# The rows of a main job are turned and split earlier, and the table of flexible jobs is built one job later

## The chip, the cores and the metric

One core of one Trainium2 chip. The metric is the device time of one execution in microseconds (us); lower is better.

## The reference

`x` is 8 x 1856 x 256. First comes a spectral layer: `X = rfft(x, axis=1)`, a complex product with `w_r + i w_i` plus biases, a soft threshold of 0.01 on the real and imaginary part, and `irfft` back to 14,848 rows of 256. Then a mixture of experts: every row picks a group of 4 and an expert in it (argmax of two small products, 16 experts in all), and its output is

```
h = np.maximum(xg[mask_e] @ w1[g, e], 0.0)      # 256 -> 1024
ye = h @ w2[g, e]                               # 1024 -> 256
out[tok_idx] = combined[:, None] * ye           # product of two softmax weights
```

## The kernel before

The spectral layer runs over four pairs of batches on TensorE, with transposes on VectorE (DVE). Each finished row is routed and scattered by GpSimd (POOL) into a list per expert in device memory, `xs_d`. Part of the experts' work (the early jobs, 256 rows each) is interleaved with the end of the spectral layer. The order of TensorE, ScalarE (ACT) and DVE there is written by hand: a string `ORDER` whose letters are steps. `D` is a second product of an early job, `E` and `J` are its output steps on ACT and DVE (lines 873 and 878), `K` the store.

After that string come 39 main jobs (`JOBS`, line 20) in one Python loop (line 1143). Three engines run in exactly the order in which the program emits their instructions; the order of the sync engine (SP), which issues the loads, is set by a scheduler. A job is one expert's rows: "l" has 384 rows, "e" 512 rows, "f" (flexible) 128 rows of an expert chosen at run time, "h" (half) two times 64 rows of two experts. Jobs 0 to 4 are l, l, l, e, l. Jobs 5, 8, 14, 23, 26, 32 and 36 are flexible; 11, 17, 29 and 35 are half jobs.

Every fp32 operand is a sum of two fp32r parts (high, low). A job goes through these steps:

- Its rows `xg` are loaded by SP (line 452). DVE turns them in 32 x 32 blocks into `x32` (line 455; the rows of the trace call this tile `x`), one buffer. `prep` then makes the high part `xth` on ACT (line 474) and the low part `xtl` on DVE (line 475). For a half job `x32` is used as it is. All this is emitted at the end of the job before (line 1191), after that job's `drain(rest)`.
- First product: `up_g` (line 480) for e and l jobs, eight slices `f` of six matmuls each (line 487). After each slice ACT makes `hh` (line 491) and DVE `hl` (line 493). Flexible jobs use `flex_mm` (line 500), with ACT's `ht`, and `flex_tr` (line 513), which turns `ht` on TensorE in two halves; ACT and DVE take `hh` and `hl` (lines 520 and 521) from it. Half jobs use `half_mm` and `half_tr` in the same way, with a plain copy on DVE (line 1099).
- Second product: `down_g` (line 545), 16 matmuls per 128 rows (lines 556 and 557), then ACT (563), DVE (564) and a store by POOL (543). It is emitted during the next job: the first two blocks of 128 rows before the next job's first product, a third or fourth one (`rest`) after it or, in flexible and half jobs, in halves between the turns.
- Meanwhile the weights of a coming job are split into high and low, eight pieces, one after each slice `f` (`todo`, lines 431 on ACT and 432 on DVE). The raw weights are loaded into two tiles `xt` (line 419); a load waits until the pieces of the tile before are done.

Which expert a flexible or half job has is written in `tab`, with the rows left in `left_of`, by `flex_table` (line 923): some 60 small DVE operations, six transposes on TensorE (line 1017), copies (1018), three small products (1029). It is a generator; four of its steps are drawn after each slice `f` of an l or e job, from job 0 on. SP reads `tab` with register loads before it can load a flexible job's weights (line 1048).

Of the kernel before, what the change touches and what calls it, by code (L numbers as in the profile page):

```python
# [10 lines left out]
F32 = mybir.dt.float32  # L11
# [18 lines left out]
NB, S, D = 8, 1856, 256  # L30
# [19 lines left out]
NF = 4  # L50
# [3 lines left out]
JOBS = _jobs()  # L54
# [103 lines left out]
def spectral_moe(ctx: ExitStack, tc: tile.TileContext, x, wri, bri, wgate, w1, w2, cst, out):  # L158
# [135 lines left out]
    def ids_of(pool, xi, w, bufs):  # L294
        both = pool.tile([128, 8], F32, name="si", bufs=bufs)
        si, gate = both[:, 4:4 + w].bitcast(I32), both[:, 0:w]
        nc.vector.tensor_scalar_add(out=si, in0=xi[:, 0:w, 0], scalar1=OFF)
        nc.vector.tensor_copy(out=gate, in_=xi[:, 0:w, 1])
        return Ids(gate, si)
# [21 lines left out]
    def bank():  # L321
        return pa.tile([128, 512], F32, name="bank")
# [32 lines left out]
    def drain(gen):  # L355
        for _ in gen:
            pass
# [103 lines left out]
    def turned(xg, n):  # L461
        xt = xq.tile([128, 2, 512], F32, name="x32", bufs=1)
        for c in range(0, n, 256):
            m = min(256, n - c)
            turn_rows(xt[:, :, c:c + m], xg, c // 32, (c + m) // 32)
        return xt

    def prep(xg, n):
        xt = turned(xg, n)
        xth = xq.tile([128, 2, 512], F32R, name="xth")  # L470
        xtl = xq.tile([128, 2, 512], F32R, name="xtl")
        for c in range(0, n, 256):
            ts = slice(c, min(n, c + 256))
            nc.scalar.copy(out=xth[:, :, ts], in_=xt[:, :, ts])  # L474
            nc.vector.tensor_tensor(out=xtl[:, :, ts], in0=xt[:, :, ts], in1=xth[:, :, ts].bitcast(F32), op=ALU.subtract)  # L475
        return xth, xtl
# [339 lines left out]

    @steps_of(range(len(jobs)))
    def e_ids(n):
        ids[n] = ids_of(early["mp"], xgs[n][1], 2, 2 * NF)

    @steps_of(range(len(jobs)))
    def e_turn(n):
# [35 lines left out]
    @steps_of(range(len(jobs)), range(2), range(2))  # L858
    def down_mm(n, t, half):
        if half == 0:  # L860
            psum["d", n, t] = early["py"].tile([128, 512], F32, name="py") if n < 2 else bank()
        o, ts = psum["d", n, t], slice(t * 128, (t + 1) * 128)
        w2b, w2h = views(wts[jobs[n][1]])[2:]
        for f in range(half * 4, half * 4 + 4):
            hh, hl = hid[n, f // 2 * 2]
            nc.tensor.matmul(o, lhsT=hh[:, f % 2, ts], rhs=w2b[:, :, f, :], start=f == 0, stop=f == 7, skip_group_check=True)
            nc.tensor.matmul(o[:, 0:D], lhsT=hl[:, f % 2, ts], rhs=w2h[:, f, :], start=False, stop=f == 7,
                             skip_group_check=True)
# [13 lines left out]
    def down_out(n, t):  # L882
# [6 lines left out]
        G=g_mm, H=g_turn, R=route_steps(), S=scatter_steps(), W=w_high, V=w_low, I=e_ids, F=e_fetch, T=e_turn, X=e_high,  # L889
        Y=e_low, U=up_mm, A=up_high, B=up_low, D=down_mm, E=down_act, J=down_add, K=down_out)  # L890

    ms = ExitStack()
    with ExitStack() as ph:
        done = 0
        ms.enter_context(tc.manual_schedule(engines=engines))
        for c in ORDER.replace("\n", ""):
            next(steps[c])
            done += c == "o"
            if c == "o" and done == NP * K1:
                fwd.close()  # L900
                early["mp"] = ph.enter_context(tc.tile_pool(name="mp", bufs=1))
                yp.append(ph.enter_context(tc.tile_pool(name="yp", bufs=3)))
                early["hp"] = ph.enter_context(tc.tile_pool(name="hp", bufs=6))
                early["pp"] = ph.enter_context(tc.tile_pool(name="pp", bufs=2, space=PSUM))
                early["py"] = ph.enter_context(tc.tile_pool(name="py", bufs=1, space=PSUM))
        assert not pend and all(next(g, None) is None for c, g in steps.items() if c not in "yzS")
        held = {e: views(wts[e]) for e in HELD}
    inv.close()

# [9 lines left out]
    nflex = ft.tile([1, 1], I32, name="nflex")  # L919
    tab = ft.tile([1, 6, 128], I32, name="tab")  # L920
    left_of = ft.tile([128, 3, 128], F32, name="left_of")

    def flex_table():
        ones_f = ft.tile([128, 128], F32, name="ones_f")
# [86 lines left out]
        yield  # L1011
        nc.vector.tensor_copy(out=nflex, in_=kk[0:1, 0:1])
        yield from (None,) * 9
        for i in range(0, 6, 2):
            o = pg.tile([128, 512], F32, name="pg")
            for c in range(2):
                nc.tensor.transpose(o[0:1, c * 128:c * 128 + 128], tb[:, i + c:i + c + 1], ident)
            nc.vector.tensor_copy(out=tab[:, i:i + 2, :], in_=o[0:1, 0:256].rearrange("p (c k) -> p c k", c=2))
            yield
        o = pg.tile([128, 512], F32, name="pg")  # L1020
        dgs = []
        for c in range(3):
# [22 lines left out]
        return xg, xi, left_k  # L1045

    def flex_entry(i, k):
        return (nc.values_load(tab[:, 2 * i, k], engines=sp, min_val=0, max_val=NE - 1),
                nc.values_load(tab[:, 2 * i + 1, k], engines=sp, min_val=0, max_val=NE * CAP))

# [14 lines left out]
    def flex_ids(rows):  # L1065
# [10 lines left out]
            tb = t.bitcast(I32)  # L1076
            nc.vector.tensor_tensor(out=tb, in0=tb, in1=k, op=ALU.bitwise_and)
        return xg, ids_of(xq, xi, 1, 4)

    def half_prep(xg):  # L1080
        return turned(xg, 128)

    def half_mm(xt, wt, hts):
        for q in range(2):
# [46 lines left out]
        s0, n = (0, EARLY) if kind == "e" else (EARLY, STAT - EARLY)  # L1131
        return (*fetch(xq, q, s0, n, 2, 4), n)

    def prep_job(j, xg, n):
        return half_prep(xg) if JOBS[j][0] == "h" else prep(xg, n)

    dma_next()
    table = flex_table()
    with ms:
        prev = None  # L1140
        xg, jids[0], n = rows_of(0)
        x2 = prep_job(0, xg, n)
        for i, (kind, q) in enumerate(JOBS):
            ids, n = jids[i], jids[i].n * 128
            if kind in "el" and i not in jw:
                jw[i] = jw[i - 1] if JOBS[i - 1] == ("e", q) else held[q]
            wt = jw[i]
            if i + 2 < len(JOBS) and JOBS[i + 2][0] == "h":
                k = JOBS[i + 2][1] + KF - KH
                jw[i + 2], rows[i + 2] = half_load(slice(k, k + 1))  # L1150
            nxt = rows_of(i + 1) if i + 1 < len(JOBS) else None
            if nxt:
                jids[i + 1] = nxt[1]
            rest = iter(())
            if prev is not None:
                if prev[3] == "h":
                    half_down(prev[0], prev[1], prev[2], "out")
                else:
                    down(psy, "py", prev[0][0], prev[1][0], prev[2], "out")
                    if len(prev[1]) > 1:  # L1160
                        rest = down_g(psy, "py", prev[0][1], prev[1][1], prev[2], "out")
            todo = []
            if i in split_at:
                jw[split_at[i]], todo = split_w(raws.pop(split_at[i]))
            hts = []
            if kind == "h":
                hs = hq.tile([128, 8 * 256 + 64], F32, name="hh")[:, 0:8 * 256].rearrange("p (f t) -> p f t", f=8)
                drain(half_mm(x2, wt, hts))
                next(rest, None)
                half_tr(hts[0], 0, hs)  # L1170
                next(rest, None)
                half_tr(hts[1], 1, hs)
            elif kind == "f":
                hs = h_tiles(n)
                for _ in flex_mm(x2, wt, hts):
                    emit(todo, 2)
                flex_tr(hts[0], 0, hs[0])
                next(rest, None)
                flex_tr(hts[1], 1, hs[0])
            else:  # L1180
                hs = h_tiles(n)
                for _ in up_g(psh, x2, n, wt, hs):
                    emit(todo, 1)
                    drain(islice(table, 4))
            emit(todo, len(todo))
            if i in split_at:
                dma_next()
            drain(rest)
            prev = (hs, ids if kind == "h" else [ids.cut(c, min(c + 2, ids.n)) for c in range(0, ids.n, 2)], wt, kind)
            if nxt is not None:  # L1190
                x2 = prep_job(i + 1, nxt[0], nxt[2])
        for h2, ids in zip(prev[0], prev[1]):
            down(psy, "py", h2, ids, prev[2], "out")

    nfx = nc.values_load(nflex[:, 0:1], min_val=0, max_val=128)  # L1195
    with tc.For_i(KF, nfx, 1) as iv:
        rw, rw_rows = flex_load(bass.ds(iv, 1))
        wt, todo = split_w(rw)
        emit(todo, len(todo))
        hts, hs = [], h_tiles(128)  # L1200
        xg, ids = flex_ids(rw_rows)
        drain(flex_mm(prep(xg, 128), wt, hts))
        for q in range(2):
            flex_tr(hts[q], q, hs[0])
        down(psy, "py", hs[0], ids, wt, None)
        wt, rw_rows = half_load(bass.ds(iv, 1))
        hts, h = [], hq.tile([128, 8 * 256 + 64], F32, name="hh")[:, 0:8 * 256].rearrange("p (f t) -> p f t", f=8)
        xg, ids = flex_ids(rw_rows)
        drain(half_mm(half_prep(xg), wt, hts))
        for q in range(2):  # L1210
            half_tr(hts[q], q, h)
        half_down(h, ids, wt, None)
# [37 lines left out]
```

## Time and profile before

| | us |
|---|---|
| median of 3 runs (1189.3 to 1198.6) | 1190.08 |
| the profiled execution | 1195.48 |
| its span in the trace | 1193.6 |
| TensorE busy in the span | 1149.6 (96%) |
| DVE busy | 791.7 (66%) |
| ACT busy | 672.9 (56%) |

The profiled execution is 1.9 us longer than its span, and 0.45% above the median. The main jobs take the time from 551 us to the end. Matmuls overlap, and their ends are modelled, so a step between two starts says more than one duration. [...]

### The profile page before, as it was taken

The page shows a single profiled execution, that of the slowest core. Times are in us where ns is not written, and L with a number is a line of the kernel's source. Part 1 is how long each engine was busy: PE and PEld are TensorE (multiplying, and loading weights), DVE is VectorE, ACT ScalarE, POOL GpSimd, SP SyncE. Part 2 cuts the span into 40 slices and gives each one's busy share as a digit, 9 for nine tenths or more (in the row PEclk, how much of TensorE's full clock was granted, in tenths as well). Part 3 has the DMA queues.
Part 4 walks back from the last instruction along what each step waited for, and adds up shares of the span by engine and source line. Part 5 has one row for each costly group of instructions (what it writes and reads, how often), then busy time and mean ns, then how long its engine had stood idle before and what let it go on. Part 6 is the DMA issues. An engine that isn't in the chain of part 4 may idle for free. (4 is left out here: it accounts for less than half of the span.)

```text
span 1193.6 us, 20882 instructions
## 1 busy us (share of the span) xinstructions
PE 1149.6 (96%) x7428; PEld 990.6 (83%) x7428; DVE 791.7 (66%) x1806; ACT 672.9 (56%) x1506; POOL 261.9 (22%) x257
## 2 busy tenths in 40 slices
PE   8999999999999889998899999999999999999997
PEld 5988889897889569887889888888898898798776
DVE  4449676978787778845785845846767566475542
ACT  2777867685778565534364734634546455454432
POOL 1000013503533532561112111111111111111101
PEclk9999999999999999999999999999999999999989
DMA  9872114103311255443353554454434356455200
GB/s 387 327 279 85 37 34 139 66 1 118 118 38 38 66 135 136 142 145 95 96 177 120 150 202 133 120 230 130 121 113 135 110 174 195 118 177 195 102 10 28
DMA packets 114602, 155.82 MB, mean 131 GB/s; under 512 B 89274, under 2 KB 90045, under 8 KB 104000
## 3 DMA queue, kind: packets, MB, share of 16 engines
q1 hardware_dynamic: 95616, 104.33, 28.7%
q0 software_dynamic: 12048, 30.67, 6.9%
q10 hardware_dynamic: 6832, 19.47, 4.2%
q8 instruction: 59, 0.97, 0.3%
q14 instruction: 47, 0.39, 0.1%
HBM read 104.47 MB, written 52.46 MB: 131 GB/s over the span
## 5 line engine op out<-in xcount | busy, mean ns | idle before, releaser
L556 PE MATMUL py<-big,hh 128*128 128x512 f32 x824 | 289.6, 394 | 0.0
L487 PE MATMUL ph<-xth,big 128*128 128x384 f32 (+1 forms) x896 | 255.5, 361 | 4.0 <-ACT xth L474 3.4
L543 POOL DMA_INDIRECT out_dram<-yo,si x123 | 119.8, 974 | 568.7 <-DVE yo L564 497.2
L557 PE MATMUL py<-big,hl 128*128 128x256 f32 x824 | 230.4, 280 | 2.5 <-DVE hl L493 2.3
L277 POOL DMA_INDIRECT xs_d<-v,sloti x128 | 138.7, 1084 | 338.9 <-ACT xh L649 154.6
L493 DVE SCALAR_TENSOR_TENSOR hl<-ph,hh 128x256 fp32r<-128x256 f32 x448 | 151.7, 380 | 62.0 <-ACT hh L491 59.7
L487 PEld LDWEIGHTS ph<-xth,big 128*128 128x128 f32 x896 | 165.7, 189 | 22.5 <-ACT xth L474 6.2
L556 PEld LDWEIGHTS py<-big,hh 128*128 128x128 f32 x824 | 154.5, 187 | 35.8 <-issue 3.2
L491 ACT ACTIVATE hh<-ph 128x256 fp32r<-128x256 f32 x448 | 133.9, 352 | 78.3 <-PE ph L487 74.7
L487 PE MATMUL ph<-xtl,big 128*128 128x384 f32 (+1 forms) x448 | 162.2, 362 | 2.6 <-DVE xtl L475 2.6
L557 PEld LDWEIGHTS py<-big,hl 128*128 128x128 f32 x824 | 155.5, 189 | 4.0 <-DVE hl L493 2.9
L563 ACT ACTIVATE yo<-py,si 128x256 f32<-128x256 f32 x103 | 48.8, 473 | 151.5 <-PE py L557 146.8
L564 DVE SCALAR_TENSOR_TENSOR yo<-py,si,yo 128x256 f32<-128x256 f32 x103 | 49.5, 482 | 109.5 <-ACT yo L563 108.2
L679 PE MATMUL pw<-wh,xh 128*128 128x256 f32 x480 | 120.2, 292 | 0.0
L432 DVE TENSOR_TENSOR big<-xt,big 128x512 fp32r<-128x512 f32 x168 | 114.1, 682 | 0.0
L679 PE MATMUL pw<-wl,xh 128*128 128x256 f32 x480 | 113.5, 278 | 0.0
L431 ACT CAST big<-xt 128x512 fp32r<-128x512 f32 x168 | 103.7, 621 | 0.0
L487 PEld LDWEIGHTS ph<-xtl,big 128*128 128x128 f32 x448 | 84.6, 189 | 12.8 <-DVE xtl L475 5.3
L679 PEld LDWEIGHTS pw<-wh,xh 128*128 128x128 f32 x480 | 90.8, 189 | 2.8 <-issue 2.4
L679 PEld LDWEIGHTS pw<-wl,xh 128*128 128x128 f32 x480 | 90.7, 189 | 2.6 <-issue 2.4
L692 DVE TENSOR_TENSOR big<-rp,rn 128x512 f32<-128x512 f32 x60 | 42.0, 705 | 45.1 <-ACT rp L686 34.2
L636 PEld LDWEIGHTS pg<-CF,big 128*128 128x128 f32 x480 | 63.8, 198 | 8.5 <-issue 2.7
(200 smaller groups left out, 2034.5 us busy)
## 6 DMA issues: line engine op xcount, KB each, us to landing
xt<-in_w_dram SPq DMA_DIRECT2D x50, 1024.0 KB
xs_d<-zero ACTq DMA_DIRECT2D x16, 1170.0 KB
big<-in_w_dram SPq DMA_DIRECT2D x16, 1024.0 KB
xt<-in_x_dram SPq DMA_DIRECT2D x8, 1024.0 KB
xg<-xs_d SPq DMA_DIRECT2D x64, 96.0 KB
xg<-xs_d SPq DMA_DIRECT2D x48, 128.0 KB
big<-in_x_dram SPq DMA_DIRECT2D x4, 1024.0 KB
v<-in_x_dram SPq DMA_DIRECT2D x4, 1024.0 KB
```

The source lines that it names most:

```text
L277: ins = nc.gpsimd.indirect_dma_start(out=xs_d, out_offset=bass.IndirectOffsetOnAxis(ap=sl_, axis=0), in_=row, in_offset=None, bounds_check ...
L431: nc.scalar.copy(out=wt[:, 2 * i, cs], in_=raws[i][:, cs])
L432: nc.vector.tensor_tensor(out=wt[:, 2 * i + 1, cs], in0=raws[i][:, cs], in1=wt[:, 2 * i, cs].bitcast(F32), op=ALU.subtract)
L487: nc.tensor.matmul(o[:, :n], lhsT=a_[:, ch, fs], rhs=b_[:, ch, 0:n], start=k == 0, stop=k == 5)
L491: nc.scalar.activation(out=hh[:, f, :m], in_=ov, func=AF.Relu)
L493: nc.vector.scalar_tensor_tensor(out=hl[:, f, :m], in0=ov, scalar=0.0, in1=hh[:, f, :m].bitcast(F32), op0=ALU.max, op1=ALU.subtract)
L543: ins = nc.gpsimd.indirect_dma_start(out=out, out_offset=bass.IndirectOffsetOnAxis(ap=ids.si[:, t:t + 1], axis=0), in_=ysb, in_offset=None ...
L556: nc.tensor.matmul(o, lhsT=hh[:, f, ts], rhs=w2b[:, :, f, :], start=f == 0, stop=f == 7, skip_group_check=True)
L557: nc.tensor.matmul(o[:, 0:D], lhsT=hl[:, f, ts], rhs=w2h[:, f, :], start=False, stop=f == 7, skip_group_check=True)
L564: nc.vector.scalar_tensor_tensor(out=ysb, in0=o[:, 0:D], scalar=gate_w, in1=ysb, op0=ALU.mult, op1=ALU.add)
L636: nc.tensor.matmul(o[:, m * 128:(m + 1) * 128], lhsT=zys[pr][:, k, ch * 128:(ch + 1) * 128, bt], rhs=T_v[:, k, :], start=True, stop=True)
L679: nc.tensor.matmul(y[:, bt * D:(bt + 1) * D], lhsT=a_[:, bt * 2 + ch, cs], rhs=w_[:, ri, ch, :], start=False, stop=fin, skip_group_check=True)
```

## The change

1. `prep` is taken apart into `turned` (DVE's turn) and `parts` (`xth`, `xtl`).
2. The last two output steps of the early jobs (`EJKEJK`) are cut off from the string and emitted after job 0's turn and split. The products that they read lie in `pg` banks now.
3. In a flexible job the next job's turn is emitted after `flex_mm`, and its split between the two `flex_tr`. In a half job both are emitted after `half_mm`.
4. `flex_table` is drawn from job 1 on instead of job 0; two copies of `tab` instead of three.

```diff
-    def prep(xg, n):
-        xt = turned(xg, n)
+    def parts(xt, n):
         xth = xq.tile([128, 2, 512], F32R, name="xth")
...
-            psum["d", n, t] = early["py"].tile([128, 512], F32, name="py") if n < 2 else bank()
+            psum["d", n, t] = (early["py"].tile([128, 512], F32, name="py") if n < 2 else
+                               pg.tile([128, 512], F32, name="pg") if n == len(jobs) - 1 else bank())
...
+    order = ORDER.replace("\n", "")
+    tail = order.rindex("D") + 2
+    assert order[tail - 1:] == "KEJKEJK"
...
-        for c in ORDER.replace("\n", ""):
+        for c in order[:tail]:
...
-        for i in range(0, 6, 2):
+        for i, n in ((0, 4), (4, 2)):
             o = pg.tile([128, 512], F32, name="pg")
-            for c in range(2):
+            for c in range(n):
...
-    def prep_job(j, xg, n):
-        return half_prep(xg) if JOBS[j][0] == "h" else prep(xg, n)
+    def prep_job(j, xt, n):
+        return xt if JOBS[j][0] == "h" else parts(xt, n)
...
-        x2 = prep_job(0, xg, n)
+        x2 = prep_job(0, turned(xg, n), n)
+        for c in order[tail:]:
+            next(steps[c])
...
-            hts = []
+            hts, x2n = [], None
             if kind == "h":
...
                 drain(half_mm(x2, wt, hts))
+                x2n = prep_job(i + 1, turned(nxt[0], nxt[2]), nxt[2])
                 next(rest, None)
...
                 for _ in flex_mm(x2, wt, hts):
                     emit(todo, 2)
+                xt = turned(nxt[0], nxt[2])
                 flex_tr(hts[0], 0, hs[0])
+                x2n = prep_job(i + 1, xt, nxt[2])
                 next(rest, None)
...
                     emit(todo, 1)
-                    drain(islice(table, 4))
+                    drain(islice(table, 4 if i else 0))
...
             if nxt is not None:
-                x2 = prep_job(i + 1, nxt[0], nxt[2])
+                x2 = prep_job(i + 1, turned(nxt[0], nxt[2]), nxt[2]) if x2n is None else x2n
```

What this moves at three places. First DVE at the end of the early jobs, before:

```order
L855 SCALAR_TENSOR_TENSOR hl<-ph,hh 128x512 x4
L878 SCALAR_TENSOR_TENSOR yo<-bank,si,yo 128x256 x4
L297 TENSOR_SCALAR si<-xi 128x3
L298 COPY si<-xi 128x3
L455 STREAM_TRANSPOSE x_6837<-xg 128x8x2x32
L455 STREAM_TRANSPOSE x_6837<-xg 128x4x2x32
L475 TENSOR_TENSOR xtl<-x_6837,xth 128x2x256
L475 TENSOR_TENSOR xtl<-x_6837,xth 128x2x128
L297 TENSOR_SCALAR si<-xi 128x3
```

and the same place now (`x_6837` and `x_6825` are job 0's `x32`; lines are those of the changed file, one or a few off):

```order
L854 SCALAR_TENSOR_TENSOR hl<-ph,hh 128x512 x4
L878 SCALAR_TENSOR_TENSOR yo<-bank,si,yo 128x256 x2
L297 TENSOR_SCALAR si<-xi 128x3
L298 COPY si<-xi 128x3
L455 STREAM_TRANSPOSE x_6825<-xg 128x8x2x32
L455 STREAM_TRANSPOSE x_6825<-xg 128x4x2x32
L474 TENSOR_TENSOR xtl<-x_6825,xth 128x2x256
L474 TENSOR_TENSOR xtl<-x_6825,xth 128x2x128
L878 SCALAR_TENSOR_TENSOR yo<-pg,si,yo 128x256 x2
L297 TENSOR_SCALAR si<-xi 128x3
```

Job 0's turn and low part have moved ahead of the last two outputs.

Second, DVE in the first flexible job (job 5), whose successor is job 6; before:

```order
L564 SCALAR_TENSOR_TENSOR yo<-py,si,yo 128x256 x2
L521 TENSOR_TENSOR hl<-ph,hh 128x4x128 x2
L564 SCALAR_TENSOR_TENSOR yo<-py,si,yo 128x256
L455 STREAM_TRANSPOSE x_8034<-xg 128x8x2x32 x2
L475 TENSOR_TENSOR xtl<-x_8034,xth 128x2x256 x2
```

and now:

```order
L563 SCALAR_TENSOR_TENSOR yo<-py,si,yo 128x256 x2
L455 STREAM_TRANSPOSE x_7995<-xg 128x8x2x32 x2
L520 TENSOR_TENSOR hl<-ph,hh 128x4x128
L474 TENSOR_TENSOR xtl<-x_7995,xth 128x2x256 x2
L520 TENSOR_TENSOR hl<-ph,hh 128x4x128
L563 SCALAR_TENSOR_TENSOR yo<-py,si,yo 128x256
```

The turn stands ahead of the first `hl`, the low part between the two. ACT's two `xth` moved in the same way between its two `hh`.

Third, ACT from the last half job (35) over flexible job 36 to job 37; before:

```order
L1091 ACTIVATE ht<-ph 128x512 x2
L563 ACTIVATE yo<-py,si 128x256
L431 CAST big<-xt 128x512 x8
L474 CAST xth<-x_13378 128x2x128
L1108 ACTIVATE yo<-py,si 128x256
L509 ACTIVATE ht<-ph 128x512 x2
L520 CAST hh<-ph 128x4x128 x2
L474 CAST xth<-x_13450 128x2x256 x2
```

and now (`x_13325` is job 36's, `x_13434` job 37's):

```order
L1095 ACTIVATE ht<-ph 128x512 x2
L473 CAST xth<-x_13325 128x2x128
L562 ACTIVATE yo<-py,si 128x256
L431 CAST big<-xt 128x512 x8
L1112 ACTIVATE yo<-py,si 128x256
L508 ACTIVATE ht<-ph 128x512 x2
L519 CAST hh<-ph 128x4x128
L473 CAST xth<-x_13434 128x2x256 x2
L519 CAST hh<-ph 128x4x128
```

Job 36's high part went ahead of the eight pieces of job 37's weights.

## Rows read from the trace of the kernel before

**Rows 1.** The page: busy time by engine, and granted clock in 40 slices.

```profile
PE 1149.6 (96%) x7428; PEld 990.6 (83%) x7428; DVE 791.7 (66%) x1806; ACT 672.9 (56%) x1506; POOL 261.9 (22%) x257
...
PEclk9999999999999999999999999999999999999989
```

**Rows 2.** Timeline, start of job 0: start us, us, engine, line, tiles [idle before, releaser].

```profile
551.46 0.48 DVE L878 SCALAR_TENSOR_TENSOR yo<-bank,si,yo 128x256 f32<-128x256 f32 x1 [2.32 <-ACT yo L873]
...
552.00 1.03 DVE L455 STREAM_TRANSPOSE x<-xg 128x512 f32<-128x512 f32 x2
...
553.39 1.03 DVE L475 TENSOR_TENSOR xtl<-x,xth 128x512 fp32r<-128x512 f32 x2 [0.36 <-ACT xth L474]
...
553.71 0.44 PE L487 MATMUL ph<-xth,big 128*128 128x384 f32 x1 [2.80 <-ACT xth L474]
```

**Rows 3.** Windows: stretch, us, busy PE PEld DVE ACT POOL, PEclk, DMA share, GB/s.

```profile
538.00:545.00 7.00, 5.77 (x39) 5.28 (x40) 2.54 (x4) 2.16 (x4) 0.53 (x1) 1.00 0.65 126
553.70:557.60 3.90, 3.57 (x11) 3.32 (x12) 1.40 (x7) 1.06 (x3) 0.00 (x0) 0.56 0.71 136
557.60:564.10 6.50, 6.50 (x39) 6.50 (x38) 6.29 (x29) 6.00 (x18) 0.00 (x0) 1.00 0.00 0
599.70:604.00 4.30, 4.30 (x26) 3.92 (x25) 3.66 (x10) 2.56 (x8) 0.00 (x0) 1.00 0.69 244
...
1134.40:1141.30 6.90, 5.96 (x16) 4.67 (x16) 1.02 (x5) 1.75 (x4) 0.97 (x1) 0.51 0.01 3
```

**Rows 4.** Timeline, DVE and TensorE, job 0's first product and the second after it.

```profile
557.06 0.62 DVE L493 SCALAR_TENSOR_TENSOR hl<-ph,hh 128x256 fp32r<-128x256 f32 x2 [2.50 <-ACT hh L491]
...
569.06 0.67 DVE L493 SCALAR_TENSOR_TENSOR hl<-ph,hh 128x256 fp32r<-128x256 f32 x2
...
564.14 0.39 PE L556 MATMUL py<-big,hh 128*128 128x512 f32 x1
...
567.76 0.39 PE L557 MATMUL py<-big,hl 128*128 128x256 f32 x1 [1.12 <-DVE hl L493]
...
569.53 0.39 PE L557 MATMUL py<-big,hl 128*128 128x256 f32 x1 [1.15 <-DVE hl L493]
```

**Rows 5.** Timeline, DVE in job 2, slices that split weights without table steps.

```profile
597.62 0.61 DVE L493 SCALAR_TENSOR_TENSOR hl<-ph,hh 128x256 fp32r<-128x256 f32 x2
...
602.14 0.62 DVE L493 SCALAR_TENSOR_TENSOR hl<-ph,hh 128x256 fp32r<-128x256 f32 x2
```

**Rows 6.** Timeline, TensorE at the table's transposes (job 1), SP at job 5's raw weights.

```profile
582.21 0.38 PE L1017 MATMUL pg<-K,fx_b 128*1 128x128 f32 x2 [1.18 <-DVE tab L1018]
...
599.68 4.37 SPq L419 DMA_DIRECT2D xt<-in_w_dram  x2
```

**Rows 7.** Timeline, DVE, then TensorE, flexible job 5 and the start of job 6.

```profile
651.93 0.69 DVE L521 TENSOR_TENSOR hl<-ph,hh 128x512 fp32r<-128x512 f32 x1 [2.89 <-ACT hh L520]
...
655.42 1.29 DVE L455 STREAM_TRANSPOSE x<-xg 128x512 f32<-128x512 f32 x2
656.86 1.30 DVE L475 TENSOR_TENSOR xtl<-x,xth 128x512 fp32r<-128x512 f32 x2
...
656.99 0.28 PE L557 MATMUL py<-big,hl 128*128 128x256 f32 x1
657.42 0.50 PE L487 MATMUL ph<-xth,big 128*128 128x512 f32 x1
...
658.55 0.39 PE L487 MATMUL ph<-xth,big 128*128 128x512 f32 x1
```

**Rows 8.** Waits: engine, what, for whom, us in total, times, longest.

```profile
DVE hh L1099 <- PE ph L1098: 18.5, 4, 4.6
...
PE ph L487 <- DVE xtl L475: 2.6, 9, 0.3
```

**Rows 9.** Timeline, DVE and TensorE, from half job 35 to flexible job 36.

```profile
1129.60 4.90 DVE L432 TENSOR_TENSOR big<-xt,big 128x512 fp32r<-128x512 f32 x8
...
1135.34 1.22 PE L506 MATMUL ph<-big,xth 128*128 128x512 f32 x2 [3.25 <-ACT xth L474]
```

**Rows 10.** Timeline, TensorE in the early jobs, an idle stretch of like length.

```profile
538.68 0.39 PE L845 MATMUL ph<-xth,big 128*128 128x256 f32 x1 [2.61 <-issue]
```

More of the change, by code (lines that the diff above doesn't have):

```diff
@@ L818, in e_ids @@
     def e_ids(n):
-        ids[n] = ids_of(early["mp"], xgs[n][1], 2, 2 * NF)
+        ids[n] = ids_of(ix, xgs[n][1], 2, 2 * NF)
     @steps_of(range(len(jobs)))
@@ L905, in spectral_moe @@
                 early["py"] = ph.enter_context(tc.tile_pool(name="py", bufs=1, space=PSUM))
-        assert not pend and all(next(g, None) is None for c, g in steps.items() if c not in "yzS")
+        assert not pend and all(next(g, None) is None for c, g in steps.items() if c not in "yzSEJK")
         held = {e: views(wts[e]) for e in HELD}
@@ L921, in spectral_moe @@
     left_of = ft.tile([128, 3, 128], F32, name="left_of")
+    made = []
     def flex_table():
@@ L1013, in flex_table @@
         yield from (None,) * 9
-        for i in range(0, 6, 2):
+        for i, n in ((0, 4), (4, 2)):
             o = pg.tile([128, 512], F32, name="pg")
-            for c in range(2):
+            for c in range(n):
                 nc.tensor.transpose(o[0:1, c * 128:c * 128 + 128], tb[:, i + c:i + c + 1], ident)
-            nc.vector.tensor_copy(out=tab[:, i:i + 2, :], in_=o[0:1, 0:256].rearrange("p (c k) -> p c k", c=2))
+            nc.vector.tensor_copy(out=tab[:, i:i + n, :], in_=o[0:1, 0:n * 128].rearrange("p (c k) -> p c k", c=n))
             yield
+        made.append(tab)
         o = pg.tile([128, 512], F32, name="pg")
@@ L1047, in flex_entry @@
     def flex_entry(i, k):
+        assert made, "the table is read before it is written"
         return (nc.values_load(tab[:, 2 * i, k], engines=sp, min_val=0, max_val=NE - 1),
@@ L1078, in flex_ids @@
         return xg, ids_of(xq, xi, 1, 4)
-    def half_prep(xg):
-        return turned(xg, 128)
     def half_mm(xt, wt, hts):
@@ L1141, in spectral_moe @@
         xg, jids[0], n = rows_of(0)
-        x2 = prep_job(0, xg, n)
+        x2 = prep_job(0, turned(xg, n), n)
+        for c in order[tail:]:
+            next(steps[c])
+        assert all(next(steps[c], None) is None for c in "EJK")
         for i, (kind, q) in enumerate(JOBS):
@@ L1201, in spectral_moe @@
         xg, ids = flex_ids(rw_rows)
-        drain(flex_mm(prep(xg, 128), wt, hts))
+        drain(flex_mm(parts(turned(xg, 128), 128), wt, hts))
         for q in range(2):
@@ L1208, in spectral_moe @@
         xg, ids = flex_ids(rw_rows)
-        drain(half_mm(half_prep(xg), wt, hts))
+        drain(half_mm(turned(xg, 128), wt, hts))
         for q in range(2):
```

## The prediction

> **What bounds the kernel now.** I read the page first, then the windows, the timelines at the borders between jobs, and the waits. TensorE is busy 96% of the span [rows 1], and through long stretches of the main jobs its clock stands at 1.00. So a gain can only be TensorE time lost now: idle time before a matmul, and work done at half clock. In the main jobs I find it at few places. At the start of job 0 TensorE is idle for 2.80 us, then the clock is at 0.56 in the window 553.7 to 557.6 [rows 2, 3]. In the second product behind job 0 there are two gaps of 1.12 and 1.15 us, both ended by DVE's `hl` [rows 4]. At the table's transposes there is one of 1.18 us [rows 6]. At nine job starts TensorE waits for `xtl` [rows 8]; by the timeline these are jobs 0, 1, 37 and the six successors of flexible jobs 5, 8, 14, 23, 26 and 32. Before job 36 stands the longest gap, 3.25 us [rows 9], followed by a window at 0.51 [rows 3]. Elsewhere in the main jobs the timeline has only pauses under half a microsecond, so ACT and DVE have time to spare but are served in a bad order.
>
> **The change, part by part.**
>
> *Job 0's rows.* DVE's turn at 552.00 stands behind two outputs, the second of which waits 2.32 us for a product that TensorE has only just ended (551.46); turn, high part and low part then take until 554.4 [rows 2]. Job 0's rows are no reason for that: 384 x 256 x 4 bytes are 0.39 MB, and in 538 to 545 the DMA engines moved 126 GB/s x 7 us = 0.88 MB [rows 3], enough for jobs 0 and 1; the turn row shows no wait for a load. In the new order the 2.4 us of work fall into DVE's idle time before the last output, while TensorE is still on the last early products. These now lie in `pg`, so that job 0's banks don't wait for the late outputs. What is late next is nothing up to the first `hh`. TensorE's last product ended at 553.71 - 2.80 = 550.91; job 0's first product ended when the next began, at 564.14 [rows 2, 4]: 13.2 us. At full clock 39 matmuls took 6.50 us, 0.167 each [rows 3]; 48 take 8.0. Gain 5.2 us, of which the half clock is 0.44 x 3.9 = 1.7. Bounds: 5.2, and 2.4 if the whole idle time stayed.
>
> *Table out of job 0.* DVE's `hl` came every (569.06 - 557.06) / 7 = 1.71 us [rows 4]; in job 2, where weights are split without table steps, every (602.14 - 597.62) / 4 = 1.13 [rows 5]. So four table steps cost 0.58 us a slice, and over seven slices the last `hl` is 4.1 us less late. The second product will want it 2.4 us sooner after the job's start (8.0 instead of 564.14 - 553.71 = 10.4), and the first `hl` comes about 1 us sooner since the first slice runs at full clock. 4.1 + 1 - 2.4 = 2.7, more than the gaps' 2.27: both go. I take 2.3; bounds 0.8 and 2.3.
>
> *Table in jobs 1 and 2.* In job 1 no weights are split, so a slice costs DVE about what it costs TensorE (6 x 0.167 = 1.0): hidden. The rest now falls on job 2, where weights are split: four slices at 1.71 against TensorE's 1.0, then the copies of `tab`. The 1.18 us in job 1 [rows 6] goes. Some 21 small steps (sixteen table steps, two copies, three scaled identities) at 0.58 / 4 are 3.0 us more on DVE in job 2; their cover is the four product banks, the `rest` product and the first two blocks of job 3's start. Job 3's split may come late through them. If all is covered, +1.2; if nothing, 1.2 - 3.0 = -1.8; I take 0, near the middle, since a slice's excess of 0.7 for four slices just fills the banks. SP is touched as well: job 5's raw weights were asked for at 599.68, in the middle of job 2 [rows 6], and now `tab` exists only at its end. One tile takes 4.3 us (244 GB/s x 4.3 us = 1.05 MB, [rows 3]); it is wanted after the first slice of job 3, behind `rest` and two blocks of second product, 48 matmuls of 0.22 and 0.11, some 8 us. Covered; if that cover is gone, up to 4.3 us.
>
> *Turns inside flexible jobs.* In job 5 DVE is idle for 2.89 us before the first `hl` [rows 7]; the turn takes 1.29 and fits. ACT then makes `xth` while TensorE does half of the `rest`. The low part, 1.30, comes between the two `hl`; the second `hl` gets later by some 0.2 us, and the product that wants it stands behind the other half of `rest`. At job 6 the last product's matmul starts at 656.99 and the third of the first product at 658.55 [rows 7]. Without waiting it would be 656.99 + 0.11 + 2 x 0.22 = 657.54 (0.167 scaled to 512 and 256 columns): 1.0 us lost. Six such starts: 6.0. Bounds: 3 (half hidden) and 6.6.
>
> *Turns inside half jobs.* `x32` has one buffer, and a half job's matmuls read it, so the next turn waits for them; behind it on DVE stand the copies of `half_tr`. DVE is idle up to 4.6 us before those copies [rows 8], against a moved 1.29 + 1.30. Jobs 11, 17 and 29 are followed by starts that lose next to nothing: 0, between +0.5 and -2.
>
> *Job 35 to 36 to 37.* Job 36's turn stood behind eight pieces of weights, 4.90 us from 1129.60 [rows 9]; now it is ahead of them. The 3.25 us go, and with them the half clock: from 1135.34 to 1141.3 at 0.51 [rows 3] 2.9 us were lost. What is late next is job 36's first `hl`: it now stands behind job 37's turn (1.29), which can't start before the pieces end at 1134.5. TensorE wants it at about 1136.1, it is there at about 1134.5 + 0.2 + 1.3 + 0.7 = 1136.7, and the second one behind the low part costs as much again; half of that was lost there before. 6.2 - 0.6 = 5.6; bounds 2.7 and 6.2.
>
> The clock is the part that I trust least. Before 553.71 and 1135.34 an idle stretch of 2.80 and 3.25 us is followed by half clock; before 538.68 one of 2.61 us is not: 538 to 545 is at 1.00 [rows 10, 3]. [...]
>
> Sum: 5.2 + 2.3 + 0 + 6.0 + 0 + 5.6 = 19.1 us. From the profiled execution's 1195.48 us (span 1193.6 and 1.9 around it) that leaves 1176.4, 1.6% less. The median before is 1190.08, 0.45% below that execution; the same share of it gives 1171.
>
> **The rivals.** *The half clock stays* where the idle time goes, or moves to another short gap, as at job 36, where I still expect gaps of half a microsecond. For it: the row of 538.68, which shows idle time and clock apart. Against it: both low windows begin within an idle stretch that the change ends. Then 1.7 + 2.9 are not gained: 14.5, or 1175.6.
>
> *The table takes over.* DVE's lag in job 2 and the late raw weights of job 5 hold ACT in job 3. For it: 1.71 against 1.0 us a slice. Against it: the 8 us of products in front. Price 4.3 us: 1175.3.
>
> *Job 0's rows aren't early.* The high part's memory was used by tiles of the early jobs, and waits for their stores would keep it back to where it was. For it: the tiles share space with a pool that is closed there. Against it: in the rows it started 0.7 us after its turn. The 2.80 us idle and the clock behind it stay, 4.5 us: 1175.5.
>
> *Slower.* In the eleven flexible and half jobs the moved turn and low part (1.29 + 1.30) stand ahead of `hl` or of half jobs' copies, and TensorE's next product waits for these. It decides if a turn starts after the idle time of 2.89 us is used up, since its rows or the one `x32` buffer come late: then up to 2.6 us are exposed at each place and the six times 1.0 are lost too. 11 x 2.6 = 29 against 5.2 + 2.3 + 5.6 = 13: 16 us slower, 1206. Against it: the idle times of 2.89 and 4.6, and that no turn in these rows waits for a load.
>
> **How the numbers follow.** Forecast 0.67, half clock 0.13, table 0.10, job 0's rows 0.07, slower 0.03. The forecast's bounds sum from 2.4 + 0.8 - 1.8 + 3 - 2 + 2.7 = 5.1 to 5.2 + 2.3 + 1.2 + 6.6 + 0.5 + 6.2 = 22.0, or 1185 to 1168; all low ends together are unlikely, and the span of three runs before (1189.3 to 1198.6) adds some at either end. I give 1164 to 1181, which takes in the three middle cases. About 1% (11.9 us) is what a measurement can tell from no change. Faster by more: 0.62 of the forecast's 0.67, and about 0.22 of the three cases near 14.5, together 0.84; within 1%: 0.13; slower by more: 0.03.
>
> **What would show it.** Right: the first matmul of job 0 follows the last early product without idle time and at clock 1.00; no gap before `hl` in the second product behind job 0; `xtl` waits at the six successors gone; job 36 starts behind the half product at once. Wrong: ACT waiting for raw weights in job 3, gaps before `hl` inside jobs 5 to 36, or a low clock in windows where nothing was idle. A median above 1181 would mean that at least two of the large terms did not come.

## The result, and the profile after

| | median us | runs |
|---|---|---|
| before, in the same session | 1191.7 | 1189.3 to 1198.6, six runs |
| after | 1177.59 | 1171.81 to 1179.53, six runs |
| ratio | 0.9866 | 95% interval 0.9831 to 0.9902 |

The kernel became 1.3% faster, 14 us. The forecast was 1171.0 with a range of 1164 to 1181: the median lies in the range, 6.6 us above the forecast. The profiled execution took 1179.42 us with a span of 1177.6, 16.0 less than the span before.

The page of the changed kernel, busy time and granted TensorE clock (PEclk; 1.00 is the full one):

```profile
PE 1144.0 (97%) x7428; PEld 990.7 (84%) x7428; DVE 790.5 (67%) x1805; ACT 672.3 (57%) x1506; POOL 260.2 (22%) x257
...
PEclk9999999999999999999999999999999999999999
```

TensorE does the same 7428 matmuls, and is busy 5.6 us less than in [rows 1]. What TensorE still waits for from job 0 on is in the view of waits of the changed kernel, 553 to 1178 us (us in total, times, longest):

```profile
PE ph L486 <- ACT xth L473: 2.0, 1, 2.0
PE py L555 <- DVE yo L563: 0.4, 1, 0.4
PE py L556 <- DVE hl L520: 0.4, 2, 0.2
PE ph L486 <- DVE xtl L474: 0.3, 1, 0.3
PE ph L516 <- ACT ht L508: 0.3, 1, 0.3
```

The nine waits for `xtl` of [rows 8] are one now, `hl` of the full jobs [rows 4] and the wait at the transposes [rows 6] are gone, and so is the 3.25 before job 36 [rows 9], whose first matmuls now start without idle time:

```profile
1122.03 0.73 PE L505 MATMUL ph<-big,xth 128*128 128x512 f32 x2
```

One large wait is left, the first line: 2.0 us for job 0's `xth`. That is one of the three places from which I expected most. The trace shows why; the timeline of the changed kernel, SP, DVE and TensorE at the start of job 0:

```profile
546.83 0.38 SPq L445 DMA_DIRECT2D xi<-xs_d  x1
...
547.26 2.08 SPq L452 DMA_DIRECT2D xg<-xs_d  x4
...
551.95 1.04 DVE L455 STREAM_TRANSPOSE x<-xg 128x512 f32<-128x512 f32 x2 [2.92 <-DMA xg<-xs_d]
...
553.67 0.44 PE L486 MATMUL ph<-xth,big 128*128 128x384 f32 x1 [2.04 <-ACT xth L473]
```

In [rows 2] the turn stood behind an output. Now it is ahead of it as planned, and waits for its own rows, whose load was issued at 547.26. Job 0 starts at 553.67 against 553.71. The half clock is there as well, and the other place of the two is clean (windows, columns as in [rows 3]):

```profile
553.70:557.60 3.90, 3.59 (x11) 3.33 (x12) 2.24 (x9) 1.71 (x5) 1.95 (x2) 0.60 0.74 136
1122.00:1129.00 7.00, 6.30 (x32) 4.68 (x31) 6.49 (x15) 4.29 (x9) 1.99 (x1) 1.00 0.01 3
```

Where the time went is read by laying the start of each job's first product (up) and second product (down) in the two traces side by side. Every step of the difference over 0.15 us behind it, taken from TensorE's timelines:

```
place                       before     after    step
job 0, up                   553.71    553.67   -0.04
job 0, down                 564.14    564.27   +0.17
job 1, up                   572.58    569.82   -2.89
job 1, down                 583.49    578.14   -2.59
job 3, up                   609.32    604.76   +0.71
job 3, down                 620.26    616.41   +0.71
jobs 6, 9, 15, 24, 27, 33   up and down        -5.9 (-0.9 each, once -1.2)
job 36, up                 1135.34   1122.03   -3.31
job 36, down               1142.21   1126.29   -2.62
job 37, up and down                            -0.1
end                        1193.64   1177.59  -16.05 in all
```

The start of job 6 shows the small term. DVE's timeline of the changed kernel in flexible job 5, then TensorE at the border:

```profile
645.11 1.29 DVE L455 STREAM_TRANSPOSE x<-xg 128x512 f32<-128x512 f32 x2
648.08 0.69 DVE L520 TENSOR_TENSOR hl<-ph,hh 128x512 fp32r<-128x512 f32 x1 [1.68 <-ACT hh L519]
648.69 1.28 DVE L474 TENSOR_TENSOR xtl<-x,xth 128x512 fp32r<-128x512 f32 x2
649.89 0.68 DVE L520 TENSOR_TENSOR hl<-ph,hh 128x512 fp32r<-128x512 f32 x1
```

```profile
653.14 0.28 PE L556 MATMUL py<-big,hl 128*128 128x256 f32 x1
653.26 0.40 PE L486 MATMUL ph<-xth,big 128*128 128x512 f32 x1
653.50 0.40 PE L486 MATMUL ph<-xtl,big 128*128 128x512 f32 x1
653.74 0.63 PE L486 MATMUL ph<-xth,big 128*128 128x512 f32 x2
```

The turn uses DVE's idle time before the first `hl` (1.68 are left of the 2.89 of [rows 7]), the low part is done at 650.0, and the second matmul of job 6 finds it ready 3.5 us later. From 653.14 to the third matmul at 653.74 are 0.60 us, against 1.56 in [rows 7].

### The profile page after: what moved, and what is told of

Same layout as the page of the kernel before. It is cut to its first block, busy times and chain, and to the rows that moved or that the text cites. A ratio compares the mean times of both kernels' runs of the same rounds, so it can differ in the third digit from the quotient of the medians.

```text
span 1177.6 us, 20877 instructions
## 1 busy us (share of the span) xinstructions
PE 1144.0 (97%) x7428; PEld 990.7 (84%) x7428; DVE 790.5 (67%) x1805; ACT 672.3 (57%) x1506; POOL 260.2 (22%) x257
## 5 line engine op out<-in xcount | busy, mean ns | idle before, releaser
L277 POOL DMA_INDIRECT xs_d<-v,sloti x128 | 136.3, 1065 | 349.4 <-ACT xh L648 154.7
## 6 DMA issues: line engine op xcount, KB each, us to landing
v<-in_x_dram SPq DMA_DIRECT2D x4, 1024.0 KB, 14.2
```

The source lines that it names most:

```text
L277: ins = nc.gpsimd.indirect_dma_start(out=xs_d, out_offset=bass.IndirectOffsetOnAxis(ap=sl_, axis=0), in_=row, in_offset=None, bounds_check ...
```

## The experiments

Eleven runs were made. A label with e is the changed kernel with at most one edit (e0_after has none, e6_again repeats e4_fly3). A label with f has three row scatters on their way at a time and at most one edit more; f0_before is the kernel before, the other f runs are the changed kernel.

**First set: is job 0's term absent, and why?** The kernel sends rows to the lists in `xs_d` by 128 indirect DMAs on GpSimd (L277). `FLY = 2` (L46) makes each one wait until the one two before it has landed. Job 0's rows can be loaded only behind the last of them. GpSimd's last scatter in the two profiled executions, of before, then of after:

```profile
536.28 0.97 POOL L277 DMA_INDIRECT xs_d<-v,sloti  x1 [0.30 <-issue]
```

```profile
544.21 0.97 POOL L277 DMA_INDIRECT xs_d<-v,sloti  x1 [0.30 <-issue]
```

It came 7.9 us later. Is this the change, or the execution?

e0_after: the changed kernel again, no edit.

> The changed kernel again, for a second profiled execution. Theory A (the last row scatter decides): job 0's loads are issued when the last scatter has landed. If GpSimd issues the last scatter before about 541 us, job 0's turn is done by 551, its first matmul starts within 0.5 us of the last early product, the clock stays at 1.00 from 551 to 558, and the time is near 1172; if it issues it after 543, the first matmul starts near 553.7, half clock follows, and the time is near 1178. Theory B (the six runs differ for some other reason, such as clock drops in the early stage): start of job 0 and total time don't go together. Median by either 1177, single runs from 1171 to 1180.

Measured: 1177.44 us (1172.03 to 1181.95), ratio to before 0.9877 [0.9842, 0.9912]. The profiled execution was one near 1172, span 1170.3:

```profile
546.14 1.04 DVE L455 STREAM_TRANSPOSE x<-xg 128x512 f32<-128x512 f32 x2 [2.95 <-DMA xg<-xs_d]
...
547.86 0.44 PE L486 MATMUL ph<-xth,big 128*128 128x384 f32 x1 [0.87 <-ACT xth L473]
```

The last scatter was issued at 537.63, and job 0 started 5.8 us earlier than in the first profile with 0.87 us idle and no half clock behind it: its first `hl` comes at 550.40, 2.54 us after the first matmul, against 3.35 in [rows 2, 4]. So in these two executions start and total go together, as theory A says; but the early products had ended earlier too (547.0 against 551.6), and the turn still waited for its rows. Of the 5.8 us, 4.6 are the early stage itself, which differs from execution to execution.

e1_tail:

```diff
-        for c in order[:tail]:
+        for c in order:
...
-        for c in order[tail:]:
-            next(steps[c])
```

The last early products stay in `pg` in this edit.

> The changed kernel with job 0's turn and split back behind the last early outputs. Theory A: what the profiled execution of the changed kernel shows at job 0 (first matmul at 553.67 against 553.71 before) holds in most executions, so this costs 0 to 2 us in the median, 1178 to 1180, and the fast group near 1172 is gone, since the turn now stands behind the last output whatever the scatters do. Rival, my forecast's first term: the move is worth 5.2 us, and the profiled execution was the exception: 1177.6 + 5.2 = 1183.

Measured: 1176.51 us (1172.32 to 1179.4), no slower than the changed kernel. With two scatters the move of job 0's rows is worth nothing that the median shows. The rival's 1183 falls. That the group near 1172 would be gone falls too, as far as one run at 1172.32 shows it: such an execution doesn't need the early turn.

e2_table: `drain(islice(table, 4 if i else 0))` back to `4`.

> The changed kernel with the table's steps drawn from job 0 on again (four a slice). From the two traces: job 0's gaps come back (2.9 us), the transposes are again in job 1 (2.6), job 3 loses its new delay (1.4): 4.1 us slower than the changed kernel, 1181.7. Rival, my forecast: 2.3 + 0, 1179.9. Second rival: the 2.9 us behind job 0 came from the early rows and not from the table: 1178.8 and no gap of over 1 us that ends on hl in job 0.

Measured: 1179.35 us (1176.84 to 1181.8). With runs that spread over 5 to 10 us, this can't be told from 1178.8, 1179.9 or 1181.7; inconclusive by time. The trace rules out the second rival: in the second product behind job 0 TensorE again waits for `hl`, 1.04 and 1.15 us.

e4_fly3: `FLY = 2` to `FLY = 3`.

> The changed kernel with three row scatters on their way at a time instead of two. Theory A: the late scatters wait for one another's landing, so with three the last one is issued some 3 us or more earlier, job 0's turn no longer waits for its rows, its first matmul starts at 551 to 552, the clock stays at 1.00 behind it: 5 us faster than the changed kernel, 1172 in nearly all runs. Rival: the scatters are late since their packets queue behind weight loads or since GpSimd waits for what it stores; then three change nothing, job 0 starts near 553.7 and the time is 1177.

Measured: 1157.48 us (1156.86 to 1158.41), ratio to before 0.9704 [0.9675, 0.9734]: 20 us faster than the changed kernel, four times what I expected, and all six runs within 1.6 us. Page and TensorE's waits from 530 us on, of this kernel:

```profile
PE 1135.3 (98%) x7428; PEld 985.0 (85%) x7428; DVE 790.6 (68%) x1805; ACT 673.4 (58%) x1506; POOL 263.4 (23%) x257
...
PEclk9999999999999999999999999999999999999998
```

```profile
PE py L555 <- DVE yo L563: 0.4, 1, 0.4
PE ph L516 <- ACT ht L508: 0.3, 1, 0.3
PE py L556 <- DVE hl L520: 0.2, 1, 0.2
```

Job 0 begins at 533.55, 20.1 us earlier, without idle time and at clock 1.00 (windows, to be held against the 0.60 above):

```profile
529.21 1.04 DVE L455 STREAM_TRANSPOSE x<-xg 128x512 f32<-128x512 f32 x2
```

```profile
533.50:537.40 3.90, 3.90 (x25) 3.90 (x24) 2.65 (x9) 3.08 (x10) 0.98 (x1) 1.00 0.34 89
```

I had expected a start at 551 to 552. Of the 20.1 us only the 2.0 of idle time are at job 0; in e4_fly3 the early products themselves end at 533.7 instead of 551.6. Of the changed kernel with two scatters, DVE and TensorE in the early stage:

```profile
208.16 2.92 DVE L718 STREAM_TRANSPOSE v<-bank 128x512 f32<-128x512 f32 x3 [4.45 <-DMA xs_d<-v,sloti]
...
211.66 0.50 PE L326 MATMUL bank<-sl,tph 128*128 128x512 f32 x1 [1.82 <-DVE sl L593]
...
448.13 0.17 DVE L297 TENSOR_SCALAR si<-xi 128x2 int32<-128x2 f32 x1 [4.46 <-DMA xi<-xs_d]
448.37 1.71 PE L749 MATMUL bank<-K,v 128*128 128x128 f32 x8 [3.64 <-ACT v L741]
```

DVE may not write the next rows into `v` before the scatters have read the last ones, and the early jobs' loads wait for scatters as well. Loads of weights stand behind such loads on SP: the one at 439.12 had waited 15.4 us for scatters, weights were issued behind it at 440.95, ACT had to wait for these until 446.70, and TensorE then for ACT. At the two places shown TensorE idles for 1.8 and 3.6 us. DVE's waits of the two kinds are 6.9 and 7.3 us in all up to job 0. With three on their way there are none. TensorE's idle time before job 0, without the first 1.5 us of the kernel, is 8.6 us instead of 21.8. In the changed kernel's first profile, with two, there were four stretches at a lower clock (from 213.2, 319.0, 407.7 and 448.7 on, 3.41 us at 0.50 each); in e4_fly3 there is none, and the windows 200 to 214, 304 to 324, 395 to 413 and 430 to 452 are at 1.00.

**Second set: the parts again, on a base whose runs agree.** All with `FLY = 3`; the changed kernel is then e4_fly3.

f0_before: the kernel before, with `FLY = 3` alone.

> The kernel before with three scatters on their way instead of two, nothing else. Theory A (two scatters in flight hold the early stage and blur the change; with three, each part of the change is worth what its stage shows): the early stage ends as soon as in the changed kernel with three, and the difference to that kernel (1157.5) is the whole sum of the parts, 5.2 for job 0's rows, 4.1 for the table, 5.9 for six flexible starts, 6.1 for job 35 to 37, 21.3 together: 1178.8. Rival (three scatters gain what they do because job 0's rows are turned early, so the gain is the change's): the kernel before gains only 5 to 10 from them, 1182 to 1187. Second rival (the first term is worth nothing anywhere): 1173.5.

Measured: 1178.37 us (1177.39 to 1182.36), so the whole change is worth 20.9 us here, as theory A says; both rivals fall. Three scatters alone take 14.2 us off the kernel before (1192.61 beside it), against 20.0 off the changed kernel: the limit had also hidden most of the first term.

f1_tail: the edit of e1_tail.

> The changed kernel with three scatters, and job 0's turn and split back behind the last early outputs. Theory A: job 0's rows are there in time with three scatters, so the order alone sets the start, and undoing it costs what I forecast for the first term: 2.8 idle, the half clock behind it 1.7, and the rest, 5.2 in all: 1162.7. Rival 1 (the clock doesn't fall there): the idle time alone, 2.8: 1160.3. Rival 2 (the order is worth nothing, as between the two profiled executions of before and after): 1157.5.

Measured: 1162.58 us (1161.78 to 1163.84), 5.1 us slower than e4_fly3. TensorE, and the window behind it:

```profile
536.22 0.50 PE L486 MATMUL ph<-xth,big 128*128 128x384 f32 x1 [2.80 <-ACT xth L473]
```

```profile
536.20:540.10 3.90, 3.63 (x11) 3.31 (x12) 1.40 (x6) 1.06 (x3) 0.00 (x0) 0.56 0.68 136
```

These are the 2.80 idle and the 0.56 of [rows 2, 3] again; 0.44 x 3.9 = 1.7 of clock makes 4.5, and 0.6 are `xtl` and the rest. Here the first term is what the forecast said.

f2_table: the edit of e2_table.

> The changed kernel with three scatters, and the table drawn from job 0 on. From the profile of the same edit with two scatters (gaps in job 0 +2.7, job 1 +1.2, later jobs -0.7 twice): 2.5 slower than 1157.5, 1160.0. Rival, the difference of the first two profiles (2.9 + 2.6 - 1.4, the transposes as they were before): 1161.6. Rival, no gain from the table at all: 1157.5.

Measured: 1161.47 us (1160.61 to 1165.11), 4.0 slower. The two gaps of [rows 4] are back, to the hundredth:

```profile
546.87 0.39 PE L556 MATMUL py<-big,hl 128*128 128x256 f32 x1 [1.12 <-DVE hl L492]
548.64 0.58 PE L556 MATMUL py<-big,hl 128*128 128x256 f32 x1 [1.15 <-DVE hl L492]
```

In this execution the window 549.0 to 552.5 behind them is at 0.56, 1.5 us more; the kernel before has no low clock behind the same two gaps (567.7 to 573.0 at 1.00). Later jobs take back 1.4. The time is that of the first rival, but by luck: the wait at the transposes, which that rival counted, doesn't come back.

f3_turns:

```diff
-                x2n = prep_job(i + 1, turned(nxt[0], nxt[2]), nxt[2])
...
-                xt = turned(nxt[0], nxt[2])
...
-                x2n = prep_job(i + 1, xt, nxt[2])
```

> The changed kernel with three scatters, and the turns of the next job's rows back behind the flexible and half jobs. Theory A: six starts behind flexible jobs lose 0.9 to 1.0 each again (5.9), job 36 its idle 3.2 and half clock 2.9 (6.1): 12.0 slower, 1169.5. Rival (the half clock at job 36 was a matter of the execution): the idle time returns but the clock stays at 1.00 between 1095 and 1120 us: 9, 1166.5. Rival (only one of the two groups counts): 1163.5.

Measured: 1168.33 us (1167.43 to 1169.47), 10.9 slower, between the two readings. By the stages: the six successors lose 0.9 to 1.2 each, 6.0 together; job 36 loses 3.32 at its start and 1.50 within it, and job 37 nothing more (-0.46 and +0.51): 4.9. The idle 3.25 comes back to the hundredth, and the half clock behind it for part of the stretch:

```profile
1108.91 0.73 PE L505 MATMUL ph<-big,xth 128*128 128x512 f32 x2 [3.25 <-ACT xth L473]
```

```profile
1108.90:1115.20 6.30, 6.20 (x21) 4.29 (x21) 1.13 (x4) 2.67 (x5) 0.97 (x1) 0.73 0.01 4
```

**Third set.** e5_fly4: `FLY = 4`.

> The changed kernel with four scatters on their way. Theory A: with three no idle time of TensorE above 1 us is left from 440 us on and its clock stays at 1.00 up to the last job, so a fourth finds nothing more to give: 1157.5, within 1. Rival (GpSimd still waits 26 us in all for its scatters' landing with three, and TensorE's 8.6 us of idle time before job 0 come from there): 1152 to 1155.

Measured: 1157.83 us (1157.11 to 1158.75): a fourth gives nothing, and the rival falls.

f4_copies: `for i, n in ((0, 4), (4, 2)):` to `((0, 2), (2, 2), (4, 2))`.

> The changed kernel with three scatters, and the table's six transposed columns taken over in three copies of two columns, as in the kernel before, instead of four and two. Theory A: the third bank and the third pair of transposes stand between products of job 2, whose DVE is the later engine there, and this is the 1 us that undoing the three other parts left unexplained (20.9 against 19.9): 1158.5. Rival (covered): 1157.5. Second rival (as in job 1 of the kernel before, where the gap was 1.18 and went with the merged copies): 1158.7 to 1159.0, with a gap of about a microsecond before a transpose in job 2.

Measured: 1164.05 us (1162.34 to 1164.7), 6.8 slower than e6_again beside it: all three expectations were far too low. DVE and TensorE in job 2:

```profile
574.79 0.68 DVE L432 TENSOR_TENSOR big<-xt,big 128x512 fp32r<-128x512 f32 x1
575.39 0.74 DVE L1023 CAST tab<-pg 1x256 int32<-1x256 f32 x2
```

```profile
575.85 0.58 PE L1022 MATMUL pg<-K,fx_b 128*1 128x128 f32 x2 [4.61 <-DVE tab L1023]
```

```profile
571.00:575.90 4.90, 0.29 (x4) 0.05 (x2) 4.80 (x16) 0.89 (x3) 0.00 (x0) 0.77 0.00 0
575.90:582.00 6.10, 6.10 (x25) 5.47 (x26) 2.44 (x8) 1.06 (x3) 0.00 (x0) 0.62 0.57 185
```

`pg` has two banks (L166). The third pair of transposes needs the first bank back, whose copy stands on DVE behind `hl` and pieces of weights up to 575.39. TensorE, in order, stands for 4.61 us, and the clock falls to 0.62 behind it: 4.6 + 0.38 x 6.1 = 6.9. Between the two profiles it is 6.2 from job 0's start on. With four and two columns there are two banks' worth and no such wait.

e6_again: e4_fly3 once more.

> The changed kernel with three scatters once more, beside the two others: 1157.5, within 1, all runs within 2 of one another. If it is 1160 or more, what was read from differences between calls is uncertain by as much.

Measured: 1157.25 us (1156.91 to 1158.17), ratio to before 0.9702 [0.9676, 0.9728]. It lies 0.2 from e4_fly3, the base of the f runs. The changed kernel with three scatters beats both kernels, by 3% and by 1.7%.

The parts on the quiet base: 5.1 (job 0's rows) + 4.0 (table) + 10.9 (turns) = 20.0, of 20.9 for the whole. The gap of 1.18 at the transposes [rows 6] would fit the remaining 0.9: f0_before has it, and f2_table, which keeps the merged copies, doesn't. It wasn't tried alone, and that the sum comes so near is partly luck, since f2_table's 4.0 contains the 1.5 of low clock that the profile of f0_before doesn't show there.

## Why the prediction was right or wrong

**Job 0's rows (5.2, measured about 0, and 5.1 with three scatters).** The step that failed is the sentence "Job 0's rows are no reason for that", with its ground "the turn row shows no wait for a load". The row shows only the wait that ended last. The load's own row in the kernel before would have told how near the other one was:

```profile
539.37 1.97 SPq L452 DMA_DIRECT2D xg<-xs_d  x4
```

The loads end being issued at 541.3, and in the trace after the rows are there 2.6 us behind that (549.34 to 551.95), so at about 544 here: seven us of room. But this room is the distance between the last scatter and the last early product, and each execution has another:

| execution | last scatter issued | last early product ends | between | idle before job 0 |
|---|---|---|---|---|
| before | 536.28 | 550.9 | 14.6 | 2.80 (behind an output) |
| after | 544.21 | 551.6 | 7.4 | 2.04 (rows) |
| e0_after | 537.63 | 547.0 | 9.4 | 0.87 (rows) |
| e1_tail | 540.57 | 550.0 | 9.4 | 2.80 (behind an output) |
| e2_table | 541.34 | 548.7 | 7.4 | 2.62 (rows) |
| e4_fly3 | 520.61 | 533.7 | 13.1 | 0 |

From the scatter's issue to the first matmul the trace after shows 553.67 - 544.21 = 9.5 us (e0_after 10.2): landing, two loads, the turn, the high part. What "between" lacks of that is the idle time. The one execution that I had was the one of the five with two scatters that had the most room, and by these figures the only one in which so long a chain would have been in time. My third rival, that job 0's rows aren't early, had the right outcome (4.5 not gained, 1175.5) by a wrong cause: I put it down to memory waiting for stores, and no run shows that.

**Table out of job 0 (2.3, measured 2.9).** Right: both `hl` gaps went, 2.27 us, and f2_table brings back the same two. The other 0.6 of this step shows no idle time and stays open.

**Table in jobs 1 and 2 (0, measured +1.2).** Job 1 gained 2.59, and 1.42 of it came back as later work of jobs 2 and 3. It is the upper bound, "if all is covered". But I had not priced the merged copies at all. They are why it was covered: f4_copies puts the price of leaving them out at 6.8 us, outside my bounds (-1.8). SP's raw weights for job 5, asked for at 600.75, kept nobody waiting, as I worked out.

**Flexible jobs (6.0, measured 5.9, and 6.0 in f3_turns) and half jobs (0, measured 0).** Right, by the steps given; no moved turn waited for the `x32` buffer in a way that TensorE saw.

**Job 35 to 37 (5.6, measured 6.1, and 4.9 in f3_turns).** Right. The waits for job 36's two `hl` that I priced at 0.6 are there as 0.22 and 0.16 (the 0.4 in the list of TensorE's waits); 0.31 more are a wait for ACT's `ht`, which I hadn't named. In f3_turns the term is smaller since a smaller part of the half clock came back (0.27 x 6.3 = 1.7, against 0.49 x 6.9 = 3.4 in [rows 3]).

**The clock.** I trusted it least, and at the places of the forecast I was too wary. In six profiles job 0 starts behind 2.0 to 2.8 us of idle time, and all six show a lower clock around the start (0.56, 0.60 and 0.56 over 3.9 us there in before, after and f1_tail); in the other seven it starts behind 0.9 us or none, and none does (1.00 over the same 3.9 us in e4_fly3). The 3.25 before job 36 is followed by it in all three profiles that have it (0.51 in before, 0.73 in f3_turns; f0_before is the third). So at these places the clock's share came and went with the idle time, and the rival with half clock at another place falls. It holds for these places alone. In all thirteen profiles TensorE idles 2.36 or 2.37 us before its first matmul of L714 (L715 in the kernel before), near 400 us; here of the changed kernel, then of e4_fly3, each with the window around it:

```profile
406.62 5.37 PE L714 MATMUL ph<-big,CI 128*128 128x512 f32 x8 [2.36 <-DVE big L691]
395.00:413.00 18.00, 15.45 (x92) 11.15 (x90) 11.61 (x19) 12.17 (x21) 7.67 (x8) 0.91 0.23 62
```

```profile
398.75 1.95 PE L714 MATMUL ph<-big,CI 128*128 128x512 f32 x4 [2.36 <-DVE big L691]
395.00:413.00 18.00, 13.57 (x37) 4.84 (x35) 14.53 (x19) 6.36 (x12) 8.10 (x8) 1.00 0.23 64
```

Eight profiles have a low stretch there (in the changed kernel 3.41 us at 0.50 from 407.7 on); five have none (e0_after, e4_fly3, f1_tail, f3_turns, f4_copies). e6_again, the same kernel as e4_fly3, has one from 399.6 on. So the same idle stretch is followed by it in some executions and not in others, as [rows 10] had warned (2.61 us idle, then 1.00). The starts of the low stretch at job 0 differ too: they lie from 0.7 us ahead of its first matmul (e1_tail) to 1.8 behind it (f0_before). In the kernel before it starts at 554.16, 0.45 us behind that matmul and not within the idle time, as I had written of both low windows; the one at job 36 does start within it, at 1134.42.

**From the sum to the median.** 19.1 were forecast, 16.05 came in the profiled pair: -5.2 for the first term, +0.6 and +1.2 for the table, +0.4 for the rest. The median fell by 14.1 only. Runs of the kernel with two scatters lie up to 14 us apart (before) and 10 (after), so the two or so us between the two figures can't be read further. The median, 1177.59, lies nearer to the three rivals (1175.3 to 1175.6) than to the forecast of 1171; the range held it since it was made wide enough for them.

## What to carry to other kernels

A row shows only the wait that ended last: before a waiting instruction is moved ahead of its releaser, look up when each of its other inputs was there, and how far that differs between executions. If the runs of a kernel spread by 1%, find what makes the spread (here a limit of two row scatters on their way) before tuning by single microseconds: lifting it gave 20.0 us on the changed kernel, and 14.2 on the kernel before, where the whole change had given 14.1, and only then could the parts be measured. When work is moved into a stretch where an engine already lags, count the buffers that it hands back through that engine; one too few cost TensorE 4.61 us here.

## What the runs showed of the hardware

Scatters of one row per partition took 2.4 us at least and 2.6 in the median from issue to landing, up to 7.4 (changed kernel, L277). The moving of the rows is included in these times; how they split no run here shows. What I had not expected is the size of what follows when a chain waits for two of them at a time: 20 us of 1177. In the two profiles 13 of them are TensorE's idle time before job 0 (21.8 against 8.6); the rest is matmuls that took longer, with four low stretches among them (3.41 us at 0.50 each) where e4_fly3 has none. A second thing: idle time of 2.36 or 2.37 us at the same place of the same kernel was followed by a low clock in one execution (e6_again, from 399.6 on) and not in another (e4_fly3, 395 to 413 at 1.00).
